# Exchanged attention products from the second batch on, with the exchange undone in the normalisation instead of in a second copy of the weights

## The chip, the cores and the metric

The kernel runs on one core of one Trainium2 chip. The metric is the time of one execution on the device, in microseconds. The engines are called as the profile calls them: PE (matrix products), PEld (its weight loads), ACT (activation functions), DVE (elementwise work and reductions), POOL (here mostly the issue of loads, and small elementwise work) and SP (a queue of DMA transfers). PSUM is the accumulator memory that PE writes and DVE and ACT read.

## The reference

Two layers, one behind the other. The first is an attention with a band of 32 positions to either side and 8 global positions, for 8 batches, 8 heads, 576 positions and a head dimension of 64. The second is a feed-forward layer over the 4608 tokens, with the width 512 and the inner width 2048.

```python
scores = scale * np.matmul(q, k.transpose(0, 1, 3, 2))
mask = np.abs(pos[:, None] - pos[None, :]) <= window
mask = mask | is_global[:, None] | is_global[None, :]
scores = np.where(mask, scores, -1000000000.0)
attn = softmax(scores)                      # along the keys
x = np.matmul(attn, v)                      # -> (4608, 512), heads side by side
h = x @ w_in                                # 512 x 2048
s = np.sin(alpha * h)
g = h + s * s / (alpha + 1e-09)
return (g @ w_out).astype(np.float32)       # 2048 x 512
```

## The kernel before, in words

Work goes batch by batch. For a batch `b` there is an attention stage (`attention(b)`), a first matrix stage (`gemm1(b)`, x times w_in with the sine part) and a second one (`gemm2(b)`, g times w_out). The order on every engine is the order in which the program is written out: `attention(b + 1)` follows `gemm1(b)`, and the matmuls of `gemm2` are handed out one by one by `fill(n)` between the pieces of both, to keep PE occupied. No scheduler moves anything.

In the attention two heads form a pair: one on partitions 0 to 63, one on 64 to 127. A batch has four pairs. The 576 queries are in two halves (positions 0 to 287 and 288 to 575, in each the even ones ahead of the odd ones); each half has its own PSUM bank, so that a product tile has two banks (half 0 and half 1) of 288 queries. For each pair `hp` the program writes, in this order:

- three groups of scores on PE (L740, into the two tiles of `ring`), the exponential on ACT (L748) and the mask on DVE (L751), with `fill` between the groups;
- between the second and the third group, the products of the pair before: `denominators` (L807, with a matrix of ones) into the tile `zd`, and the value products (L834) into the tile `zn`. Both are made of matmuls with 64 rows and 64 columns. For the last pair of a batch the values go into `zd` and the denominators into `zr`;
- after the third group, for the pair before: `inverse` on ACT (L860 the logarithm, L863 the exponential of its negative, into `R`), `sums` on DVE (L844, what the global rows need), and `normalise` on DVE (L866): values times `R`, from PSUM into `xT` in bfloat16.

The tiles `zn` and `zd` exist once each, so the next pair's products can be written only when the pair before has been read. `xT` has one chunk of 128 partitions for each pair, and `gemm1` takes the four chunks as its four contraction steps, the last pair's chunk last.

A *crossed* batch (`cross`) exchanges the heads of a pair in half 1: the product of the head on rows 0 to 63 goes to columns 64 to 127 and the other way round, while half 0 stays as it is:

```python
at = t ^ (half if cross else 0)
```

So the four quadrants of the PE array all have work, where a plain batch uses two. In the kernel before, batches 4 to 7 are crossed (`CROSS = 4`). For half 1 their `xT` holds the two heads in each other's places, and `gemm1` multiplies that half with `w_alt`, a copy of `w_in` whose two partition halves are exchanged. The copy is made by eight DMA transfers on SP's queue during the attention of batches 3 and 4.

The global rows of a batch are collected from `GS`, the output of `sums`, by `keep_globals` (L883, L885) and `finish_globals` (L893, L898) into extra columns of `xlast`. In a crossed batch other than the last the additions and the two last steps are on POOL and `finish_globals` is put off to the end of `gemm1`; otherwise all is on DVE. In a crossed batch the swap for half 1 is undone for these columns' sums and done again for the result.

Of the kernel before, what the change touches and what calls it, by code (L numbers as in the profile page):

```python
# [10 lines left out]
ALU = mybir.AluOpType  # L11
AF = mybir.ActivationFunctionType
DT = mybir.dt
# [3 lines left out]
P = 128  # L17
KW = 96
NG = 8
KT = 48  # L20
# [227 lines left out]
def kernel(  # L248
# [11 lines left out]
    nc = tc.nc  # L260
# [37 lines left out]
    HG = main.tile([P, NT, NG * B], DT.bfloat16, name="HG")  # L298
    identb = main.tile([P, P], DT.bfloat16, name="identb")
    ones = main.tile([P, P], DT.bfloat16, name="ones")  # L300
    w_alt = main.tile([P, CT, DFF], DT.bfloat16, name="w_alt")
    MASK = main.tile([P, NT12, WCOL], DT.bfloat16, name="MASK")
    kTg = main.tile([P, NHP, NG, B], DT.bfloat16, name="kTg")
    qTg = main.tile([P, NHP, NG, B], DT.bfloat16, name="qTg")
# [408 lines left out]
    def attention(b, beside):  # L713
# [139 lines left out]
        def body(hp, key):  # L853
            return nd(hp, key).rearrange("p k x c -> p (k x) c")[:, :, 0 : 3 * SEG].rearrange(
                "p k (m c) -> p k m c", c=SEG
            )[:, :, :, 4:]

        def inverse(hp):
# [3 lines left out]
            n = b * NHP + hp  # L862
            nc.scalar.activation(out=Rs[hp][:], in_=L[:], func=AF.Exp, scale=-1.0, accum_out=RA[:, n : n + 1])  # L863

        def normalise(hp):
            nc.vector.tensor_tensor(  # L866
                out=xT[:, hp, :, 0:HALF].rearrange("p e (k m c) -> p e k m c", k=2, c=KT) if odd
                else xT[:, hp].rearrange("p e (k m c) -> p (e k) m c", k=2, c=KT),
                in0=body(hp, 0).rearrange("p (e k) m c -> p e k m c", k=2) if odd else body(hp, 0),
                in1=Rs[hp][:].rearrange("p (e k) m c -> p e k m c", k=2) if odd else Rs[hp][:], op=ALU.mult,  # L870
            )
# [3 lines left out]
        SWAP = [(slice(0, D), slice(D, P)), (slice(D, P), slice(0, D))]  # L875

        def keep_globals(hps):

# [12 lines left out]
        def finish_globals(hps):  # L891

            nc.vector.reciprocal(out=RG[:, hps], in_=GT[:, 1, hps])  # L893
            to = xlast[:, hps, :, HALF:].rearrange("p h e (c x b) -> p h e x c b", x=2, b=B)
            for e in range(2):
                cs = slice(2 * e, 2 * e + 2)
                for mine, other in SWAP if e else [(slice(0, P), slice(0, P))]:
                    (nc.gpsimd if cross and not wide else nc.vector).tensor_tensor(  # L898
                        out=to[mine, :, e, :, :, b], in0=GT[other, 0, hps, :, cs], in1=RG[other, hps, :, cs],
                        op=ALU.mult,  # L900
                    )

        start, per_scores = (START, PER_SCORES) if b != 1 else (0, LATE)
        def idle(hp):
# [134 lines left out]
    def gemm1(b):  # L1039


        xT = xTs[b]
        r0 = (b % 2) * S
        more = b == B - 1
        W = HALF + (NE if more else 0)
        hr = tc.alloc_tile_pool(name="hr", bufs=1, space=PSUM)
        hs = {}

        order = "nrdonrdonrdnrdon" if b == 0 else "nrd" * 5 + "n"

        def chunks(nt, cs):
            if nt not in hs:
                if order[nt] == "o":
                    hs[nt] = [(slice(e, e + 1), zo[e][:, None, :]) for e in range(2)]
                else:
                    h = {"n": zn, "d": zd}.get(order[nt]) or hr.tile([P, 2, 512], DT.float32, name="zr")
                    hs[nt] = [(slice(0, 2), h[:])]
            h = [ap[:, i] for es, ap in hs[nt] for i in range(es.stop - es.start)]
            for c in cs:
                for e in range(2):  # L1060
                    lhsT = (w_alt if e and b >= CROSS else w_in)[:, c, nt * P : (nt + 1) * P]
                    nc.tensor.matmul(  # L1062
                        out=h[e][:, 0:W], lhsT=lhsT, rhs=xT[:, c, e, 0:W],
                        start=(c == 0), stop=(c == CT - 1), skip_group_check=True,
                    )

        on_act = (ON_ACT_FIRST, ON_ACT_SECOND, ON_ACT)[min(b, 2)]
        for nt in range(NT):
            if b < 2 and 10 <= nt < 14:
                for which, t, y in PLACES[2 * (nt - 10) : 2 * (nt - 9)]:  # L1070
                    place(b + 1, which, t, y, nc.vector.tensor_copy, slice(0, NHP if b else 2))
            if 1 < b < B - 1 and nt in ((3, 5, 7, 9) if b == 2 else (3, 5)):
                place(b + 1, *PLACES[(nt + 5 if b == 2 else nt + 9) // 2], nc.vector.tensor_copy)
            if b == 1 and nt == 14:
                turn_qk(3)
            if b == 1 and nt in (3, 4):
                square_x(0, nt - 3)
            if b == 0 and nt == 11:
                turn_kq()
            if b == 0 and nt == 11:  # L1080

                load_w_out()
                cast_globals_v()
                place_globals(1)
                load_v(1, (2, 3))
                load_vg(1)
            if nt == 0:

                for n in range(2):
                    chunks(n, range(CT - 1))  # L1090
            chunks(nt, range(CT - 1, CT) if nt < 2 else range(CT))
            fill((GROUP_LATE if b == 1 else PER_GROUP)[nt])
            sb = spool.tile([P, 2, HALF + NE], DT.bfloat16, name="sb")
            s2 = spool.tile([P, 2, HALF + NE], DT.bfloat16, name="s2")
            for es, h in hs[nt]:
                nc.scalar.activation(  # L1096
                    out=sb[:, es, 0:W], in_=h[:, :, 0:W], func=AF.Sin, scale=alphaT[:, nt : nt + 1]
                )
            if nt in on_act:
                nc.scalar.activation(out=s2[:, :, 0:W], in_=sb[:, :, 0:W], func=AF.Square)  # L1100
            else:
                nc.vector.tensor_tensor(out=s2[:, :, 0:W], in0=sb[:, :, 0:W], in1=sb[:, :, 0:W], op=ALU.mult)  # L1102
            for es, h in hs[nt]:
                nc.vector.scalar_tensor_tensor(  # L1104
                    out=H2[:, nt, r0 : r0 + S].rearrange("p (e c) -> p e c", e=2)[:, es],
                    in0=s2[:, es, 0:HALF], scalar=recipT[:, nt : nt + 1], in1=h[:, :, 0:HALF],
                    op0=ALU.mult, op1=ALU.add,
                )
            if more:
                nc.vector.scalar_tensor_tensor(  # L1110
                    out=HG[:, nt, :].rearrange("p (x n) -> p x n", x=2),
                    in0=s2[:, :, HALF:W], scalar=recipT[:, nt : nt + 1], in1=hs[nt][0][1][:, :, HALF:W],
                    op0=ALU.mult, op1=ALU.add,
                )
        if b and later:
            later.pop()()
        hr.release()
# [54 lines left out]
            else:  # L1172
                n -= 1

    CROSS = 4
    EXCHANGE = {(CROSS - 1, 0): 0, (CROSS - 1, 2): 1, (CROSS, -1): 2, (CROSS, 1): 3}
    START = 2
    PER_SCORES = ((1, 11, 3), (3, 2, 4), (3, 3, 3), (3, 4, 4))

# [12 lines left out]
    def phase_a(b_att, b_moe):  # L1192
        def beside(at):

            if b_moe is None:
                if at == -1:
                    nc.vector.tensor_scalar(out=recipT[:], in0=alphaT[:], scalar1=1e-9, scalar2=None, op0=ALU.add)
                    nc.vector.reciprocal(out=recipT[:], in_=recipT[:])
                if at == 0:
                    second_half()  # L1200
                    nc.gpsimd.memset(VX[1][:].bitcast(DT.int32), 0)
                    nc.gpsimd.memset(QX[1][:].bitcast(DT.int32), 0)
                    nc.gpsimd.memset(KX[1][:].bitcast(DT.int32), 0)
                    turn_qk(1)
                    nc.gpsimd.tensor_copy(out=seen[:], in_=turned[1][1][0:1, 0:1])
                    load_w_in((2, 3))
                    load_v(1, (0, 1))
                    gather(v, gv)
                return
            if 0 <= at < 2 and b_moe:  # L1210
                square_x(b_moe, at)
            if b_att == 1 and at == 0:
                place_rest(1)
                place_rest(0)
            for which, t, y in places_at(b_att, at):
# [12 lines left out]

        if b_moe is not None:
            waiting.append(gemm2(b_moe))  # L1230
        attention(b_att, beside)
# [83 lines left out]
```

## Time and profile before

| | |
|---|---|
| runs shown, median (lowest to highest) | 367.36 us (366.95 to 370.75) |
| the profiled execution's own time | 367.21 us |
| its span | 365.4 us |
| granted TensorE clock, mean | 0.995 |
| PE busy | 333.7 us, 91% of the span |
| ACT busy | 292.7 us, 80% |
| DVE busy | 286.0 us, 78% |
| POOL busy | 143.6 us, 39% |
| all normalisations (L866), 32 instructions | 24.2 us |

A row of a timeline gives the start in us, the duration in us, the engine, the line, the operation, the tile it writes and those it reads, the shape and how many instructions the row merges; in brackets stands how long the engine sat idle before it and which instruction ended that. A row of groups gives the total busy time in us and the mean in ns of one instruction. A row of windows gives the stretch, its length, and the busy time and the number of instructions of each engine in it. The busy time of PE contains modelled ends, so PE can look full while it waits.

### The profile page before, as it was taken

How to read it: one execution, taken by the hardware profiler on the slowest of the kernel's cores; microseconds unless marked ns; L12 is line 12 of the kernel's file. 1: busy time of each engine (PE TensorE's matmuls, PEld its weight loads, DVE VectorE, ACT ScalarE, POOL GpSimd, SP SyncE). 2: the span in 40 equal slices, each digit the busy share in tenths (PEclk: the TensorE clock that was granted, in tenths of full speed). 3: DMA queues.
4: the chain of work that ended last, by engine and by line, in shares of the span. 5: the costliest groups of instructions: out<-in, count | busy, mean ns of one | idle time of the engine just before them, and what ended most of it. 6: DMA issues, size and time to landing. Idle time of an engine off the chain costs nothing. (4 is left out here: it accounts for less than half of the span.)

```text
span 365.4 us, 9492 instructions
## 1 busy us (share of the span) xinstructions
PE 333.7 (91%) x3516; PEld 218.6 (60%) x3568; DVE 286.0 (78%) x630; ACT 292.7 (80%) x566; POOL 143.6 (39%) x264
## 2 busy tenths in 40 slices
PE   2579878999999999999999999999999999999993
PEld 2457655666666666676656765667566655565452
DVE  5775899698878888888886888698887878788751
ACT  5689898787879878887989788979888789778711
POOL 7992577479774700762004571294100010000001
PEclk9999999999999999999999999999999999999997
DMA  7999999999999885999244993198521001100321
GB/s 125 110 169 180 170 137 170 175 139 201 171 213 205 98 122 136 158 152 168 67 104 67 180 152 69 33 87 96 111 54 35 1 31 60 31 1 2 86 88 50
DMA packets 104222, 40.23 MB, mean 110 GB/s; under 512 B 94266, under 2 KB 98378, under 8 KB 103722
## 3 DMA queue, kind: packets, MB, share of 16 engines
q0 software_dynamic: 56640, 18.56, 44.5%
q1 hardware_dynamic: 47530, 20.99, 29.8%
q8 instruction: 30, 0.49, 0.6%
q14 instruction: 22, 0.18, 0.2%
HBM read 37.15 MB, written 17.83 MB: 150 GB/s over the span
## 5 line engine op out<-in xcount | busy, mean ns | idle before, releaser
L1125 PE MATMUL zo<-w_out,H 128*128 128x512 bf16 x524 | 141.4, 379 | 1.9 <-issue 0.2
L394 POOL DMA_DIRECT2D VX<-in_v_dram x128 | 83.5, 665 | 52.1 <-PE zn L834 19.5
L1062 PEld LDWEIGHTS <-w_in 128*128 128x128 bf16 x768 | 74.8, 98 | 36.2 <-issue 7.2
L1125 PEld LDWEIGHTS <-H 128*128 128x128 bf16 x576 | 52.3, 97 | 37.4
L748 ACT ACTIVATE E<-ring 128x480 bf16<-128x480 f32 x96 | 54.4, 569 | 19.5 <-PE ring L740 19.3
L751 DVE TENSOR_TENSOR E<-E,MASK 128x480 bf16<-128x480 bf16 x96 | 36.1, 406 | 13.0 <-ACT E L748 11.1
L1104 DVE SCALAR_TENSOR_TENSOR H<-s,recipT,zn 128x576 bf16<-128x576 bf16 x47 | 38.2, 814 | 8.8 <-ACT s L1100 4.8
L1100 ACT ACTIVATE s<-sb 128x576 bf16<-128x576 bf16 (+1 forms) x62 | 42.8, 691 | 2.0
L740 PE MATMUL ring<-QX,KX 128*128 128x120 bf16 x384 | 37.4, 222 | 6.9 <-ACT E L748 2.6
L1096 ACT ACTIVATE sb<-zn,alphaT 128x576 bf16<-128x576 f32 (+1 forms) x47 | 34.9, 742 | 10.8 <-PE zn L1062 9.6
L740 PEld LDWEIGHTS <-KX 128*128 128x128 bf16 x384 | 27.4, 100 | 23.5 <-issue 6.8
L1102 DVE TENSOR_TENSOR s<-sb 128x576 bf16<-128x576 bf16 (+1 forms) x66 | 30.6, 464 | 10.4 <-ACT sb L1096 10.3
L1104 DVE SCALAR_TENSOR_TENSOR H<-s,recipT,zr 128x576 bf16<-128x576 bf16 x39 | 31.7, 814 | 4.9 <-ACT s L1100 2.6
L1104 DVE SCALAR_TENSOR_TENSOR H<-s,recipT,zd 128x576 bf16<-128x576 bf16 x39 | 31.7, 813 | 4.5 <-ACT s L1100 2.4
L1096 ACT ACTIVATE sb<-zd,alphaT 128x576 bf16<-128x576 f32 (+1 forms) x39 | 28.9, 742 | 7.8 <-PE zd L1062 7.6
L1096 ACT ACTIVATE sb<-zr,alphaT 128x576 bf16<-128x576 f32 (+1 forms) x39 | 28.9, 742 | 6.5 <-PE zr L1062 6.4
L1062 PEld LDWEIGHTS <-w_alt 128*128 128x128 bf16 x256 | 25.0, 98 | 13.2 <-issue 4.0
L1131 ACT COPY osb<-zo 128x512 f32<-128x512 f32 x36 | 20.8, 579 | 12.6 <-PE zo L1125 11.5
L1062 PE MATMUL zn<-xlast,w_in 128*128 128x288 bf16 (+1 forms) x144 | 27.0, 288 | 0.6 <-DVE xlast L898 0.3
L1062 PE MATMUL zn<-xT,w_in 128*128 128x288 bf16 x136 | 25.2, 286 | 2.2 <-DMA w_in<-in_moe_w_in_dram 1.6
L807 PEld LDWEIGHTS <-ones 64*64 64x64 bf16 x512 | 17.5, 107 | 15.9 <-issue 12.0
L1159 POOL DMA_INDIRECT out_dram<-osb,ghalf x1 | 1.1, 1106 | 63.7 <-POOLq L1283 63.7
(170 smaller groups left out, 556.5 us busy)
## 6 DMA issues: line engine op xcount, KB each, us to landing
VX<-in_v_dram POOLq DMA_DIRECT2D x128, 36.0 KB, 5.8
kd<-in_k_dram POOLq DMA_DIRECT2D x7, 576.0 KB, 6.8
qd<-in_q_dram POOLq DMA_DIRECT2D x7, 576.0 KB, 10.0
w_in<-in_moe_w_in_dram POOLq DMA_DIRECT2D x4, 512.0 KB, 6.9
w_out<-in_moe_w_out_dram POOLq DMA_DIRECT2D x4, 512.0 KB, 7.9
out_dram<-osb SPq DMA_DIRECT2D x8, 256.0 KB
w_alt<-w_in SPq DMA_DIRECT2D x8, 256.0 KB
out_dram<-osb SPq DMA_DIRECT2D x8, 224.0 KB
```

Of the source, the lines that this page charges most:

```text
L394: nc.gpsimd.dma_start(out=VX[b % 2][r : r + 24, hp], in_=v[b, 2 * hp + t].rearrange("(i a y) d -> y a i d", a=24, y=2)[y],)
L740: nc.tensor.matmul(out=ps[:, e * WCOL : (e + 1) * WCOL], lhsT=kx[:, hp, i, :], rhs=qx[:, hp, :, s0 : s0 + 60], start=True, stop=True, skip ...
L748: nc.scalar.activation(out=Eg, in_=ps[:, 0 : 4 * WCOL], func=AF.Exp, scale=scale, accum_out=EA[:, n : n + 1])
L751: nc.vector.tensor_tensor(out=Eg, in0=Eg, in1=MASK[:, 4 * g : 4 * g + 4, :].rearrange("p i c -> p (i c)"), op=ALU.mult,)
L807: nc.tensor.matmul(out=bass.AP(tensor=to.tensor, offset=to.offset, ap=[list(to.ap[0]), [SEG, len(ms)], list(to.ap[1]), [1, hi - lo]],), lh ...
L1062: nc.tensor.matmul(out=h[e][:, 0:W], lhsT=lhsT, rhs=xT[:, c, e, 0:W], start=(c == 0), stop=(c == CT - 1), skip_group_check=True,)
L1096: nc.scalar.activation(out=sb[:, es, 0:W], in_=h[:, :, 0:W], func=AF.Sin, scale=alphaT[:, nt : nt + 1])
L1100: nc.scalar.activation(out=s2[:, :, 0:W], in_=sb[:, :, 0:W], func=AF.Square)
L1102: nc.vector.tensor_tensor(out=s2[:, :, 0:W], in0=sb[:, :, 0:W], in1=sb[:, :, 0:W], op=ALU.mult)
L1104: nc.vector.scalar_tensor_tensor(out=H2[:, nt, r0 : r0 + S].rearrange("p (e c) -> p e c", e=2)[:, es], in0=s2[:, es, 0:HALF], scalar=recip ...
L1125: nc.tensor.matmul(out=ops[:], lhsT=H2[:, nt, blk * P : (blk + 1) * P], rhs=w_out[:, nt, :], start=(nt == 0), stop=(nt == NT - 1),)
L1131: nc.scalar.copy(out=osb[:], in_=ops[:])
```

## The change

`w_alt` and its eight transfers are gone, and `gemm1` uses `w_in` for both halves. `CROSS` is 1, so the batches 1 to 7 are crossed. `normalise` in a crossed batch is written as three instructions in place of one: one over all partitions for half 0, and two over 64 partitions each for half 1, which read one partition half and write the other, so that `xT` has both heads where they belong. `finish_globals` has two instructions in place of three in the crossed batches, since nothing needs to be exchanged there any more. With `CROSS`, `keep_globals` and the last steps of `finish_globals` of the batches 1 to 3 move from DVE to POOL, and the last steps to the end of `gemm1`.

```diff
-    w_alt = main.tile([P, CT, DFF], DT.bfloat16, name="w_alt")
...
+        SAME = [(slice(0, P), slice(0, P))]
+        SWAP = [(slice(0, D), slice(D, P)), (slice(D, P), slice(0, D))]
+
         def normalise(hp):
-            nc.vector.tensor_tensor(
-                out=xT[:, hp, :, 0:HALF]...,
-                in0=body(hp, 0)..., in1=Rs[hp][:]..., op=ALU.mult,
-            )
+            if not cross:
+                nc.vector.tensor_tensor(
+                    out=xT[:, hp, :, 0:HALF]...,
+                    in0=body(hp, 0)..., in1=Rs[hp][:]..., op=ALU.mult,
+                )
+                return
+            for e in range(2):
+                ks = slice(2 * e, 2 * e + 2)
+                for mine, other in SWAP if e else SAME:
+                    nc.vector.tensor_tensor(
+                        out=xT[mine, hp, e, 0:HALF].rearrange("p (k m c) -> p k m c", k=2, c=KT),
+                        in0=body(hp, 0)[other, ks], in1=Rs[hp][other, ks], op=ALU.mult,
+                    )
...
             for e in range(2):
                 cs = slice(2 * e, 2 * e + 2)
-                for mine, other in SWAP if e else [(slice(0, P), slice(0, P))]:
-                    (nc.gpsimd if cross and not wide else nc.vector).tensor_tensor(
-                        out=to[mine, :, e, :, :, b], in0=GT[other, 0, hps, :, cs], in1=RG[other, hps, :, cs],
-                        op=ALU.mult,
-                    )
+                (nc.gpsimd if cross and not wide else nc.vector).tensor_tensor(
+                    out=to[:, :, e, :, :, b], in0=GT[:, 0, hps, :, cs], in1=RG[:, hps, :, cs], op=ALU.mult
+                )
...
-                    lhsT = (w_alt if e and b >= CROSS else w_in)[:, c, nt * P : (nt + 1) * P]
+                    lhsT = w_in[:, c, nt * P : (nt + 1) * P]
...
-    CROSS = 4
-    EXCHANGE = {(CROSS - 1, 0): 0, (CROSS - 1, 2): 1, (CROSS, -1): 2, (CROSS, 1): 3}
+    CROSS = 1
...
-            if (b_att, at) in EXCHANGE:
-                c = EXCHANGE[b_att, at]
-                for t in range(2):
-                    nc.sync.dma_start(
-                        out=w_alt[t * D : (t + 1) * D, c], in_=w_in[(1 - t) * D : (2 - t) * D, c]
-                    )
```

More of the change, by code (lines that the diff above doesn't have):

```diff
@@ L863, in inverse @@
             nc.scalar.activation(out=Rs[hp][:], in_=L[:], func=AF.Exp, scale=-1.0, accum_out=RA[:, n : n + 1])
+        SAME = [(slice(0, P), slice(0, P))]
+        SWAP = [(slice(0, D), slice(D, P)), (slice(D, P), slice(0, D))]
         def normalise(hp):
[L866 to L870, printed above, removed]
-            )
+            if not cross:
+                nc.vector.tensor_tensor(
+                    out=xT[:, hp, :, 0:HALF].rearrange("p e (k m c) -> p e k m c", k=2, c=KT) if odd
+                    else xT[:, hp].rearrange("p e (k m c) -> p (e k) m c", k=2, c=KT),
+                    in0=body(hp, 0).rearrange("p (e k) m c -> p e k m c", k=2) if odd else body(hp, 0),
+                    in1=Rs[hp][:].rearrange("p (e k) m c -> p e k m c", k=2) if odd else Rs[hp][:], op=ALU.mult,
+                )
[7 more added lines that the diff above has]
+                    )
         GT, GM = [normp.tile([P, 2, NHP, 2, 4], DT.float32, name=name) for name in ("GT", "GM")]
         RG = normp.tile([P, NHP, 2, 4], DT.float32, name="RG")
-        SWAP = [(slice(0, D), slice(D, P)), (slice(D, P), slice(0, D))]
         def keep_globals(hps):
```

## The prediction

> **What bounds the kernel now.** I read the page first, for the span, then the busy time of each engine over the attention stages, then the timeline of two of those stages side by side: batch 3, the last one whose products are not exchanged, and batch 6, one of those whose products are.
>
> ```profile
> span 365.4 us, 9492 instructions
> ...
> core 0: us, PE busy (x) PEld busy (x) DVE busy (x) ACT busy (x) POOL busy (x), PEclk, DMA share, GB/s
> 137.84:157.49 19.65, 19.28 (x272) 12.37 (x275) 15.46 (x37) 16.30 (x41) 8.35 (x13) 1.00 0.78 141
> 178.04:196.18 18.14, 17.70 (x272) 10.35 (x275) 15.37 (x37) 16.48 (x41) 0.00 (x0) 1.00 0.29 76
> 254.88:273.04 18.16, 17.73 (x273) 10.35 (x276) 15.39 (x36) 16.05 (x40) 1.17 (x3) 1.00 0.42 82
> 96.79:116.92 20.13, 19.76 (x274) 12.63 (x277) 14.90 (x35) 16.31 (x42) 13.59 (x26) 1.00 1.25 201
> ```
>
> The stretches are the attention of batches 3, 4, 6 and 2. PE looks full in all, yet its busy time holds modelled ends, so the timeline decides. Batches 4 and 6 take the same time within 0.02 us; I let batch 6 stand for 4 and 5. Exchanged attention is 1.49 us shorter than plain attention (19.65 against 18.16).
>
> ```profile
> 143.73 0.79 PE L807 MATMUL zd<-E,ones 64*64 64x264 bf16 x16
> 144.35 0.79 PE L834 MATMUL zn<-E,VX 64*64 64x88 bf16 x28
> 147.64 0.76 DVE L866 TENSOR_TENSOR xlast<-zn,R 128x576 bf16<-128x576 f32 x1 [0.45 <-ACT R L863]
> 148.60 0.79 PE L834 MATMUL zn<-E,VX 64*64 64x88 bf16 x28
> 152.84 0.79 PE L834 MATMUL zn<-E,VX 64*64 64x88 bf16 x28
> 157.49 0.90 PE L1062 MATMUL zn<-xlast,w_in 128*128 128x288 bf16 x6
> ...
> 260.78 0.49 PE L807 MATMUL zd<-E,ones 64*64 64x264 bf16 x16
> 261.10 0.48 PE L834 MATMUL zn<-E,VX 64*64 64x88 bf16 x28
> 261.51 0.38 PE L740 MATMUL ring<-QX,KX 128*128 128x120 bf16 x4
> 261.93 0.57 ACT L748 ACTIVATE E<-ring 128x480 bf16<-128x480 f32 x1 [0.81 <-PE ring L740]
> 262.49 0.74 ACT L860 ACTIVATE L<-zd,tiny 128x576 f32<-128x576 f32 x1
> 263.26 0.68 ACT L863 ACTIVATE R<-L 128x576 f32<-128x576 f32 x1
> 263.26 0.23 DVE L844 TENSOR_REDUCE GS<-zd 128x16 f32<-128x64 f32 x1 [0.22 <-ACT L L860]
> 263.40 0.21 DVE L844 TENSOR_REDUCE GS<-zn 128x16 f32<-128x64 f32 x1
> 264.07 0.76 DVE L866 TENSOR_TENSOR xT<-zn,R 128x576 bf16<-128x576 f32 x1 [0.45 <-ACT R L863]
> 264.74 1.24 DVE L992 TENSOR_TENSOR SQ<-SQ 128x1152 bf16<-128x1152 bf16 x2
> 264.88 0.60 PE L834 MATMUL zn<-E,VX 64*64 64x88 bf16 x28
> 267.93 0.21 DVE L844 TENSOR_REDUCE GS<-zn 128x16 f32<-128x64 f32 x1
> 268.06 0.75 DVE L866 TENSOR_TENSOR xT<-zn,R 128x576 bf16<-128x576 f32 x1
> 268.86 0.60 PE L834 MATMUL zn<-E,VX 64*64 64x88 bf16 x28
> 273.04 0.29 PE L1062 MATMUL zn<-xT,w_in 128*128 128x288 bf16 x1
> ```
>
> The reader is to see a closed loop in batch 6. The value products (L834) write the one tile zn; the third group of scores (L740) follows on PE; ACT takes its exponential (L748), then the logarithm and the reciprocal of the denominators (L860, L863); DVE normalises out of zn (L866); only then may the next value products overwrite zn. From 261.10 on each begins within some 0.1 us of the end of the one before, and 264.07 + 0.76 = 264.83 is followed by value products at 264.88; again 268.06 + 0.75 = 268.81 and 268.86. The loop takes 3.78 us, then 3.98 us. In batch 3 the normalisation ends at 148.40 and the products begin at 148.60, when PE comes to them by itself: there PE is the bound, with 4.25 and 4.24 us from products to products. So **in the exchanged batches the normalisation is on the path that sets the end, in the plain ones it has 0.2 us to spare.** The change makes all batches from 1 on exchanged ones, and makes just this instruction longer.
>
> **The change, part by part.** *The normalisation.* One instruction over 576 elements becomes three over 288: all partitions for the first half, and two of 64 partitions for the second. No 288-wide form of it is in this trace. Its price comes from another PSUM operation that occurs in both widths:
>
> ```profile
> L866 DVE TENSOR_TENSOR xT<-zn,R 128x576 bf16<-128x576 f32 x12 | 9.1, 755 | 4.1 <-ACT R L863 4.1
> ...
> L1104 DVE SCALAR_TENSOR_TENSOR H<-s,recipT,zn 128x576 bf16<-128x576 bf16 x47 | 38.2, 814 | 8.8 <-ACT s L1100 4.8 <-PE zd L1062 0.5 <-issue 0.2
> ...
> L1104 DVE SCALAR_TENSOR_TENSOR H<-s,recipT,zo 128x288 bf16<-128x288 bf16 x6 | 2.8, 508 | 0.1
> ...
> L898 DVE TENSOR_TENSOR xlast<-GT,RG 64x8 bf16<-64x8 f32 x4 | 0.8, 190 | 0.1
> ...
> 308.08 0.60 DVE L898 TENSOR_TENSOR xlast<-GT,RG 128x8 bf16<-128x8 f32 x3
> ```
>
> Half the width saves 814 - 508 = 306 ns, so one piece takes about 755 - 306 = 449 ns; that only half of the partitions take part saves nothing, I assume. Do the pieces overlap? The two sums at 263.26 and 263.40 do: each lasts over 0.2 us and they start 0.14 us apart, 0.09 us of overlap. The L898 triple at 308.08 is one full-width piece and two that swap the partition halves: 0.60 us against 3 x 0.19, so 0.015 us of gap each and no overlap. The new triple has that shape, so I take no overlap: 3 x 0.45 + 2 x 0.015 = 1.38 us against 0.755, **0.63 us later at its end**. The instruction behind it also loses its overlap (SQ started at 264.74, before 264.83): 0.10 us of DVE more. Lower bound, with overlap: 3 x 0.45 - 2 x 0.09 = 1.17, +0.42 us. Upper bound, pieces as dear as the 508 ns row: 1.55, +0.80 us.
>
> The Trainium skill (VectorE: DVE Perf Modes, section on two Vector instructions with no wait between them) says that an instruction is held until all earlier Vector instructions have finished if its inputs or its output start in another 32-partition quadrant than the last ones did. By that rule both swapped pieces and the instruction after them are held, and the triple at 308.08 agrees with it, at no overlap. The section on the errata of that page gives 120 cycles plus one per element at 0.96 GHz for a PSUM source: by that estimate 425 ns a piece, 725 ns for the whole (the trace has 755), and a total near 374 us.
>
> *Batches 4 to 6.* The first loop grows by 0.63. In the second DVE has no spare time between the two normalisations (the last sum ends at 268.14, behind the start at 268.06), so the lost overlap counts too: 0.73. Then the first matrix product needs the last normalisation:
>
> ```profile
> 273.88 0.76 DVE L866 TENSOR_TENSOR xT<-zd,R 128x576 bf16<-128x576 f32 x1 [0.46 <-ACT R L863]
> ...
> 274.81 0.28 PE L1062 MATMUL zn<-xT,w_alt 128*128 128x288 bf16 x1
> ```
>
> The second half of the last chunk began at 274.81; it now waits until 273.88 + 1.38 + 0.05 = 275.31: 0.50. PE takes its work in a fixed order, so fill-in matmuls queued behind the waiting one can't cover it. Sum 1.86 a batch, **5.6 us**.
>
> *Batch 7.* Two loops at 0.63 (DVE has no SQ work there). Its gathering of the global rows stands on DVE ahead of the last normalisation:
>
> ```profile
> 312.43 0.62 DVE L898 TENSOR_TENSOR xlast<-GT,RG 128x8 bf16<-128x8 f32 x3
> 313.07 0.76 DVE L866 TENSOR_TENSOR xlast<-zd,R 128x576 bf16<-128x576 f32 x1
> 314.18 0.30 PE L1062 MATMUL zn<-xlast,w_alt 128*128 128x320 bf16 x1
> ```
>
> The triple at 312.43 loses one piece (0.2 us) and the one at 308.08 as well; the normalisation of the third pair ahead of it is longer by 0.63 and 0.10. So 313.07 moves by 0.53, its end comes at 314.98, and the product of 314.18 begins at 315.03, 0.85 late; less the 0.2 of the earlier triple, 0.65. **1.9 us.**
>
> *Batches 1 to 3* become exchanged. The denominators shrink from 0.62 (143.73 to 144.35) to 0.32 (260.78 to 261.10): -0.30. The loops become 3.78 + 0.63 = 4.41 against 4.25 and 3.98 + 0.73 = 4.71 against 4.24: +0.16 and +0.47. From the last value products into zn to the matrix product it is 4.18 (268.86 to 273.04) against 4.65 (152.84 to 157.49): -0.47. The wait for the last normalisation adds about 0.45. Together +0.31 a batch, taken three times: **0.9 us**. Half of PE's gain is given back in each loop.
>
> *What costs nothing.* Eight copies of w_in go from SP's queue; nobody waits for them until batch 4. The global rows of batches 1 to 3 move from DVE to POOL, where the copy GM waits for the sums at the end of the attention, with the casts and V loads of later batches queued behind it:
>
> ```profile
> 102.99 0.53 POOL L331 DMA_DIRECT2D kd<-in_k_dram  x1
> ...
> 126.14 2.63 POOL L394 DMA_DIRECT2D VX<-in_v_dram  x4
> 145.44 2.55 POOL L394 DMA_DIRECT2D VX<-in_v_dram  x4 [16.67 <-PE zn L834]
> ```
>
> At worst, in batch 2, the cast of 102.99 (for batch 4) waits for the end of that attention at 116.92, some 14 us, and with it the loads that ended at 128.77. But POOL then stood idle for 16.67 us, and the transpose that needs the cast is issued when the next matrix stage ends, at 137.84, some 20 us after the late cast. If that cover were short, batch 4's keys would be late by the difference. I take 0.
>
> **Sum.** 5.6 + 1.9 + 0.9 = 8.4 us on the profiled execution's own 367.2 us (its span of 365.4 and 1.8 around it; the median of the runs is 367.36, which is the same): **375.6 us**, 2.2% slower.
>
> **Rivals.** *The pieces overlap.* With 0.42 in place of 0.63 and nothing lost behind it: batches 4 to 6 3.4 (0.42 + 0.42 + 0.29 each), batch 7 1.0, batches 1 to 3 -1.3 (-0.30 - 0.05 + 0.16 - 0.47 + 0.24 each): 3.1 us, 370.3 us. For it speaks the overlap at 263.40; against it the triple at 308.08.
>
> *The exchange pays and the pieces are hidden.* If the value products started when the old normalisation would have ended (because the pieces run shorter, or only the first gates them), batches 1 to 3 would each gain the 1.49 us between the windows: 367.2 - 4.5 = 362.7 us. It decides from the point where the triple takes no longer than 0.76 + 0.2 us. Against it: the same products of batch 6 start 0.05 us after the whole normalisation. The Trainium skill (TensorEngine Tiling, on the PSUM bottleneck) has the rule behind this: packing the array speeds up TensorE but not the emptying of PSUM. The 0.05 us agree with it.
>
> *DVE becomes the bound.* It is busy 15.4 of 18.2 us in such a stage and gets 4 x 0.73 = 2.9 more: 18.3. If its order then delays the masks that all products need, all 2.9 us land on the path in seven batches, less the 4.5: 367.2 + 20.4 - 4.5 = 383.1 us. Against it: while PE waits, DVE's later work moves along with PE's.
>
> **How the numbers follow.** Forecast 0.70, overlap 0.15, hidden pieces 0.05, DVE bound 0.10. The upper bound of 0.80 us gives batches 4 to 6 7.1, batch 7 2.6, batches 1 to 3 2.5: 379.4 us. The range is 370.3 to 379.5. About 1% is what the measurement can tell from no change (363.7 to 371.0): the forecast and the DVE case lie above, half of the overlap case within. Faster 0.04, same 0.09, slower 0.87.
>
> **What would show it.** Right: triples of about 0.45 us each and 1.38 together; value products 0.05 us behind the third piece in every batch from 1 on, 4.4 and 4.7 us apart; exchanged denominators of 0.32 us from batch 1; attention stages of about 19.5 us; the second half of the first matrix product behind the last piece. Wrong: value products that start ahead of the third piece, pieces that overlap, or gaps on PE that the profile puts to POOL's loads.

## The result, and the profile after

The changed kernel takes 379.25 us (median of 6 runs, 377.54 to 380.94) where the kernel before, run beside it, takes 369.65 (366.95 to 373.83): the ratio is 1.028 with a 95% interval of 1.021 to 1.034. It is taken from the means without one run of the kernel before (373.83 us), which fell in a slower state. The forecast was 375.6 us, or +8.4; measured is +9.6 between the medians and +10.3 between the means behind the ratio. The profiled execution took 379.52 us.

The page of the changed kernel:

```profile
span 377.8 us, 9530 instructions
...
PE 332.9 (88%) x3516; PEld 213.6 (57%) x3568; DVE 299.2 (79%) x671; ACT 291.9 (77%) x566; POOL 148.6 (39%) x276
```

PE's work is as it was; the span is 12.4 us longer and DVE is busy for 13 us more. The windows of the changed kernel, with the columns of the ones shown before, over the attention of batches 3, 4, 6 and 2:

```profile
140.89:162.36 21.47, 18.41 (x272) 10.52 (x275) 17.42 (x43) 16.35 (x41) 6.19 (x14) 1.00 0.65 88
183.17:203.07 19.90, 17.91 (x273) 10.36 (x275) 17.34 (x43) 16.81 (x43) 1.99 (x4) 1.00 0.37 66
263.72:283.71 19.99, 18.00 (x273) 10.45 (x275) 17.33 (x43) 16.35 (x41) 0.81 (x2) 1.00 0.39 72
99.14:119.87 20.73, 18.44 (x275) 10.60 (x277) 16.98 (x41) 16.38 (x43) 5.91 (x11) 1.00 0.54 89
```

Batches 4 and 6 grow from 18.14 and 18.16 us to 19.90 and 19.99. Batch 2, which gained the cheaper products, still goes from 20.13 to 20.73, and batch 3 from 19.65 to 21.47. The timeline of batch 6 in the changed kernel:

```profile
273.00 1.39 DVE L879 TENSOR_TENSOR xT<-zn,R 128x288 bf16<-128x288 f32 x3 [0.45 <-ACT R L862]
...
274.42 1.25 DVE L1000 TENSOR_TENSOR SQ<-SQ 128x1152 bf16<-128x1152 bf16 x2
274.44 0.60 PE L833 MATMUL zn<-E,VX 64*64 64x88 bf16 x28 [0.61 <-DVE xT L879]
...
277.74 1.38 DVE L879 TENSOR_TENSOR xT<-zn,R 128x288 bf16<-128x288 f32 x3
279.18 0.60 PE L833 MATMUL zn<-E,VX 64*64 64x88 bf16 x28 [0.82 <-DVE xT L879]
...
282.26 1.39 DVE L879 TENSOR_TENSOR xT<-zn,R 128x288 bf16<-128x288 f32 x3 [0.45 <-ACT R L862]
...
283.71 0.90 PE L1070 MATMUL zn<-xT,w_in 128*128 128x288 bf16 x6 [0.20 <-DVE xT L879]
...
284.18 1.41 DVE L879 TENSOR_TENSOR xT<-zd,R 128x288 bf16<-128x288 f32 x3
...
285.65 0.28 PE L1070 MATMUL zn<-xT,w_in 128*128 128x288 bf16 x1 [0.18 <-DVE xT L879]
```

Each row of L879 is the three pieces together. The value products follow 0.05 and 0.06 us behind the last piece, and PE is now idle in front of them with DVE's normalisation as releaser, which before it was not. The last but one PE row is a wait that the prediction didn't name: the first matmul of the matrix product writes `zn` too, and waits for the third pair's normalisation (282.26 + 1.39 = 283.65).

To place the loss, I take in each batch the start of the second half of the last chunk in the first matrix product (285.65 above, 274.81 before), and the steps from batch to batch:

| batch | before, us | after, us | step longer by |
|---|---|---|---|
| 0 | 35.36 | 35.09 | |
| 1 | 74.44 | 76.81 | 2.64 |
| 2 | 118.52 | 121.57 | 0.68 |
| 3 | 159.08 | 164.30 | 2.17 |
| 4 | 197.78 | 204.77 | 1.77 |
| 5 | 236.28 | 245.12 | 1.85 |
| 6 | 274.81 | 285.65 | 2.00 |
| 7 | 314.18 | 326.72 | 1.70 |

Batches 4 to 7 sum to 7.3 us against 7.5 forecast; batches 1 to 3 to 5.5 against 0.9. Three parts make up most of the surplus. In batch 1 most is a wait in the matrix stage before it, for the load of `w_in`. The changed kernel's timeline:

```profile
44.14 2.10 PE L1070 MATMUL zn<-xT,w_in 128*128 128x288 bf16 x8 [2.35 <-DMA w_in<-in_moe_w_in_dram]
```

That stage (the first matrix product of batch 0) lasted 21.82 us, and 19.77 before. In the twelve experiments below it took 17.8 to 22.3 us, from 17.8 to 22.1 among the variants of the kernel before alone: the scatter of one load, not the change. It accounts for 2.05 of the 2.64 us.

In batch 2 it is a second loop of 5.10 us. The changed kernel's DVE in it:

```profile
110.22 1.25 DVE L1000 TENSOR_TENSOR SQ<-SQ 128x1152 bf16<-128x1152 bf16 x2
...
111.73 0.91 DVE L356 COPY KX<-kt 64x1152 bf16<-64x1152 bf16 x2
112.67 1.05 DVE L750 TENSOR_TENSOR E<-E,MASK 128x480 bf16<-128x480 bf16 x3
...
113.91 1.38 DVE L879 TENSOR_TENSOR xT<-zn,R 128x288 bf16<-128x288 f32 x3
```

DVE has no gap worth the name there and two key copies (L356) where the same loop of batch 6 has one. The loop is 0.36 us longer than the 4.74 us (274.44 to 279.18) of batch 6, which the prediction let stand for it; that the second copy makes the difference is read from these rows.

Batch 3 is the part that the prediction had set to zero. POOL, SP, DVE and PE in the changed kernel's timeline, in order of time:

```profile
120.33 0.51 POOL L893 COPY GM<-GS 64x64 f32<-64x64 f32 x2 [14.34 <-DVE GS L843]
...
121.18 0.59 POOL L330 DMA_DIRECT2D kd<-in_k_dram  x1
...
143.93 2.56 POOL L393 DMA_DIRECT2D VX<-in_v_dram  x4
```

```profile
122.63 9.74 SPq L402 DMA_DIRECT2D VX<-VGb  x8
...
134.65 6.27 SPq L339 DMA_TRANSPOSE kt<-kd  x1
141.02 4.77 SPq L339 DMA_TRANSPOSE qt<-qd  x1
```

```profile
146.28 0.96 DVE L356 COPY KX<-kt 64x1152 bf16<-64x1152 bf16 x2 [2.47 <-DMA kt<-kd]
147.27 1.05 DVE L750 TENSOR_TENSOR E<-E,MASK 128x480 bf16<-128x480 bf16 x3
148.05 0.73 PE L806 MATMUL zd<-E,ones 64*64 64x264 bf16 x12 [1.05 <-DVE E L750]
```

And SP in the kernel before:

```profile
119.76 6.14 SPq L403 DMA_DIRECT2D VX<-VGb  x8
...
131.56 3.20 SPq L340 DMA_TRANSPOSE kt<-kd  x1
134.88 2.55 SPq L340 DMA_TRANSPOSE qt<-qd  x1
```

`GM` waits for the end of batch 2's attention, and with it the cast at 121.18, which before was issued at 102.99. The V loads whose issue used to end at 128.77 are now issued until 146.49, so SP's two transposes run beside loads from POOL's queue, and their rows last 6.27 and 4.77 us instead of 3.20 and 2.55. DVE comes to its key copy 2.47 us before the keys have landed; masks and denominators stand behind it, and PE has 1.05 us of idle time in front of the denominators. From the last matmul of the matrix stage to the first value products (the head of a batch, below) it is 7.81 us, 6.64 before, and 6.34 in the exchanged batches 4 and 6.

### The profile page after: what moved, and what is told of

Read it like the earlier page. It is cut to its first block, busy times and chain, and to the rows that moved or that the text cites. A ratio compares the mean times of both kernels' runs of the same rounds, so it can differ in the third digit from the quotient of the medians.

```text
span 377.8 us, 9530 instructions
## 1 busy us (share of the span) xinstructions
PE 332.9 (88%) x3516; PEld 213.6 (57%) x3568; DVE 299.2 (79%) x671; ACT 291.9 (77%) x566; POOL 148.6 (39%) x276
## 5 line engine op out<-in xcount | busy, mean ns | idle before, releaser
L1070 PEld LDWEIGHTS <-w_in 128*128 128x128 bf16 x1024 | 99.7, 98 | 54.6 <-issue 15.0
L393 POOL DMA_DIRECT2D VX<-in_v_dram x128 | 83.5, 664 | 32.8 <-DMA qd<-in_q_dram 10.3
L1104 ACT ACTIVATE sb<-zn,alphaT 128x576 bf16<-128x576 f32 (+1 forms) x47 | 34.8, 740 | 15.3 <-PE zn L1070 15.3
L1104 ACT ACTIVATE sb<-zd,alphaT 128x576 bf16<-128x576 f32 (+1 forms) x39 | 28.9, 740 | 7.9 <-PE zd L1070 7.9
L893 POOL COPY GM<-GS 64x64 f32<-64x64 f32 x12 | 3.3, 274 | 79.9 <-DVE GS L843 79.7
L1104 ACT ACTIVATE sb<-zr,alphaT 128x576 bf16<-128x576 f32 (+1 forms) x39 | 28.9, 740 | 7.2 <-PE zr L1070 7.0
L1070 PE MATMUL zn<-xT,w_in 128*128 128x288 bf16 x184 | 28.3, 293 | 3.7 <-DMA w_in<-in_moe_w_in_dram 2.3
L1070 PE MATMUL zn<-xlast,w_in 128*128 128x288 bf16 (+1 forms) x192 | 29.5, 289 | 2.2 <-DVE xlast L879 1.2
L833 PEld LDWEIGHTS <-VX 64*64 64x64 bf16 x896 | 17.5, 109 | 13.4 <-issue 13.3
```

Source lines behind the costliest of these rows:

```text
L393: nc.gpsimd.dma_start(out=VX[b % 2][r : r + 24, hp], in_=v[b, 2 * hp + t].rearrange("(i a y) d -> y a i d", a=24, y=2)[y],)
L833: nc.tensor.matmul(out=out_t[at * D : (at + 1) * D, half, :, a - half * CUT : z - half * CUT], lhsT=VXb[rows, hp, i, :], rhs=E[rows, i, :, ...
L1070: nc.tensor.matmul(out=h[e][:, 0:W], lhsT=lhsT, rhs=xT[:, c, e, 0:W], start=(c == 0), stop=(c == CT - 1), skip_group_check=True,)
L1104: nc.scalar.activation(out=sb[:, es, 0:W], in_=h[:, :, 0:W], func=AF.Sin, scale=alphaT[:, nt : nt + 1])
```

## The experiments

"Before" below is the kernel before run on the same chip beside each experiment (medians 368.71, 368.75 and 368.02 us in the three groups of four). Loops are counted from the start of one pair's value products to the next's.

### The changed kernel, exchanging from batch 4

```diff
-    CROSS = 1
+    CROSS = 4
```

> The changed kernel with the exchange from batch 4 on again (batches 1 to 3 plain, with one normalisation instruction and their global rows on DVE); w_alt stays out and batches 4 to 7 keep the three-piece normalisation. My theory (the longer normalisation lies in the loop of products and normalisation): batches 4 to 7 cost 7.3 us as in the profile after (1.8, 1.9, 2.0, 1.7 from the second half of one first matrix product to the next), batches 1 to 3 nothing: about +7.5 us on the kernel before, and no DVE wait for the key transposes in batch 3. Rival (the exchange in the early batches is what costs, through DVE's total load or the tiles' new addresses): about +3 us or less. Rival (new addresses alone): as slow as the changed kernel, +10.

Measured: 374.88 us, ratio 1.017 (1.013 to 1.021). In the profile the steps of batches 4 to 7 are 40.47, 40.32, 40.66 and 41.07 us, together 7.4 longer than before, and those of batches 1 to 3 are as before within 0.3 us (39.09, 44.06, 40.89). So in the profile the pieces cost what was forecast for them, and the rest is in batches 1 to 3. Between the medians it is 6.2 us (4.9 to 7.6 by the interval).

### The changed kernel with the old layout of memory

```diff
+    w_alt = main.tile([P, CT, DFF], DT.bfloat16, name="w_alt")
```

> The changed kernel with the tile w_alt still allocated and not used, so that all tiles lie where they lay in the kernel before. My theory (addresses play no part; the 2 us that the first matrix stage of batch 0 took longer in the profile after, waiting for w_in, are chance): as slow as the changed kernel within 1 us, about 2.7% slower than the kernel before. Rival (the shift of the tiles by 16 KB slows the transposes and the loads of batch 0): 2 us faster than the changed kernel, and the first matrix stage of batch 0 takes 19.8 us again instead of 21.8.

Measured: 378.6 us, ratio 1.027 (1.023 to 1.031), and the stages are those of the changed kernel, 7.82 us at the head of batch 3 included. No effect of the addresses is seen. Beside the run above on the same chip, it puts a number on batches 1 to 3 that doesn't hang on one profile: 378.6 - 374.88 = 3.7 us.

### The changed kernel with the global rows of batches 1 to 3 on DVE

```diff
-            eng = nc.gpsimd if cross and not wide else nc.vector
+            eng = nc.gpsimd if cross and not wide and b >= 4 else nc.vector
```

(and the same condition at the two other places, L896 and L907)

> The changed kernel, but the global rows of batches 1 to 3 are collected and finished on DVE at once, as in the kernel before; POOL has only its loads there. My theory of the part that I missed (POOL holds the casts and loads of batches 4 and 5 until the sums of batch 2 are there, so the key transposes of batch 4 come late and DVE waits 2.5 us for them in batch 3, with the masks queued behind): this wait goes, batch 3 gets about 1.2 us faster than in the changed kernel, the whole 0.5 to 1.5 us, since DVE has some 1.4 us more at the end of three batches. Rival (the transposes are slow because of the traffic or the addresses, not because of POOL's order): the wait stays and the time is the same or slower.

Measured: 377.29 us, ratio 1.024 (1.020 to 1.028). Its profile, SP in batch 3:

```profile
124.25 6.15 SPq L402 DMA_DIRECT2D VX<-VGb  x8
...
136.42 2.93 SPq L339 DMA_TRANSPOSE kt<-kd  x1
```

The transposes are short again (that of the queries takes 2.01 us), DVE has no wait for the keys in the view of waits, and the head of batch 3 takes 6.34 us instead of 7.81. So the move to POOL is what made batch 3 late: 1.47 us there. In the runs only 1.3 of 3.7 us come back (378.6 to 377.29; the intervals overlap), since the rows on DVE delay the sine part: the matrix stage of batch 2 takes 21.44 us instead of 20.91.

### Three pieces for the first pair alone, and for the third alone

The kernel before, where one chunk of `xT` is written unexchanged in three pieces and multiplied with `w_in`:

```diff
+    THREE = (0,)        # (2,) in the second kernel
...
+            if cross and hp in THREE:
+                ... three pieces as in the change
...
-                    lhsT = (w_alt if e and b >= CROSS else w_in)[:, c, nt * P : (nt + 1) * P]
+                    lhsT = (w_alt if e and b >= CROSS and c not in THREE else w_in)[:, c, nt * P : (nt + 1) * P]
```

> The kernel before (exchange from batch 4 on, w_alt kept), with the three-piece normalisation for the first pair only of batches 4 to 7; the first chunk of the product then takes w_in for both halves, and the global rows have one more small instruction. My theory (place decides: the next value products wait for this normalisation): first to second value products 4.4 us instead of 3.8, the others as before, +0.65 to +0.75 us a batch, +2.8 us in all. Rival (DVE's load decides): the same cost for the first and the third pair.

> As the run before it, with the three pieces for the third pair only. No value products wait for this pair's normalisation; only the first matmul of the matrix stage does, which uses the same PSUM tile and had 0.3 us to spare. My theory: third value products to matrix stage 4.5 us instead of 4.2, all else as before, +0.35 us a batch and some 0.5 in batch 7 (global rows), +1.5 us in all, half of the first pair's cost. Rival (DVE's load decides): the same as for the first pair, +2.8 us.

Measured: 371.72 us, ratio 1.008 (1.005 to 1.012), and 371.3 us, 1.006 (1.003 to 1.010). The times alone can't tell the two apart; the profiles can. The first pair alone, batch 6:

```profile
266.85 1.39 DVE L873 TENSOR_TENSOR xT<-zn,R 128x288 bf16<-128x288 f32 x3 [0.26 <-ACT R L863]
...
268.29 0.60 PE L834 MATMUL zn<-E,VX 64*64 64x88 bf16 x28 [0.62 <-DVE xT L873]
...
272.40 0.60 PE L834 MATMUL zn<-E,VX 64*64 64x88 bf16 x28 [0.19 <-DVE xT L878]
```

The loop with the three pieces takes 4.41 us, the one behind it 4.11 (268.29 to 272.40) instead of 3.98: 0.63 and 0.13, as the prediction had it with 0.63 and 0.10. The steps of batches 4 to 7 grow by 0.69, 0.73, 0.74 and 0.64, 2.8 us in all. The third pair alone, batch 6:

```profile
271.90 0.60 PE L834 MATMUL zn<-E,VX 64*64 64x88 bf16 x28
...
274.99 1.40 DVE L873 TENSOR_TENSOR xT<-zn,R 128x288 bf16<-128x288 f32 x3 [0.45 <-ACT R L863]
...
276.43 0.28 PE L1081 MATMUL zn<-xT,w_in 128*128 128x288 bf16 x1 [0.20 <-DVE xT L873]
```

Both loops stay at 3.77 and 3.98, and the matrix product starts 4.53 us behind the value products (271.90 to 276.43) instead of 4.18. The steps grow by 0.53, 0.41, 0.15 and 0.43, 1.5 us in all. So the wait of the matrix product for `zn` is real, and the third pair pays for its pieces there.

### Three pieces that exchange nothing

The kernel before, with each exchanged batch's normalisation in three pieces whose output is on the partitions of the input:

```diff
+            if cross:
+                for e, rows in ((0, slice(0, P)), (1, slice(0, D)), (1, slice(D, P))):
+                    ks = slice(2 * e, 2 * e + 2)
+                    nc.vector.tensor_tensor(
+                        out=xT[rows, hp, e, 0:HALF]...,
+                        in0=body(hp, 0)[rows, ks], in1=Rs[hp][rows, ks], op=ALU.mult,
+                    )
+                return
```

> The kernel before, with every normalisation of batches 4 to 7 in three pieces of the same sizes that don't change partitions: all partitions, 0 to 63, 64 to 127; w_alt kept. By the Trainium skill's rule on held Vector instructions (VectorE: DVE Perf Modes) the second piece is not held and the third one is: 0.45 + 0.45 + 0.45 - 0.09 + 0.015, 1.28 us, against 1.39 us for the exchanging pieces. If the exchange itself cost something, the pieces would be shorter than 0.45 us. If pieces never overlap whatever their partitions, 1.39 us. Loops 0.5 us longer than in the kernel before, +6 us in all.

Measured: 373.96 us, ratio 1.014 (1.008 to 1.020). Three views of one triple in its timeline (the first window ends behind the first piece, the second begins ahead of the second piece, the third holds all three), and the group's rows (64 and 128 partitions):

```profile
269.44 0.46 DVE L869 TENSOR_TENSOR xT<-zn,R 128x288 bf16<-128x288 f32 x1 [0.45 <-ACT R L863]
```

```profile
269.82 0.91 DVE L869 TENSOR_TENSOR xT<-zn,R 64x288 bf16<-64x288 f32 x2
```

```profile
269.44 1.29 DVE L869 TENSOR_TENSOR xT<-zn,R 128x288 bf16<-128x288 f32 x3 [0.45 <-ACT R L863]
```

```profile
L869 DVE TENSOR_TENSOR xlast<-zn,R 64x288 bf16<-64x288 f32 x12 | 5.4, 450 | 0.1
...
L869 DVE TENSOR_TENSOR xlast<-zn,R 128x288 bf16<-128x288 f32 x6 | 2.7, 456 | 1.6 <-ACT R L863 1.5
```

The second piece starts at 269.82, 0.08 us before the first has ended (269.90). The two 64-partition pieces take 0.91 us, twice the group's mean of 450 ns and a gap. The whole is 1.29 us where the exchanging triple takes 1.38 to 1.41. The Trainium skill (VectorE: DVE Perf Modes, section on two Vector instructions with no wait between them) holds an instruction back whose inputs or output start in another 32-partition quadrant than the last ones. By that rule the second piece here isn't held and the third is, and this trace agrees: one overlap of 0.08, then none. The missing overlap is worth about 0.1 us. The other 0.53 of the 0.63 us (1.29 against 0.76) is the splitting itself. The loops are 4.30 and 4.75: the first is 0.11 us shorter than with the exchanging pieces, the second (4.74 there) is not, and why isn't settled.

### The inverse ahead of the third scores, in the changed kernel and in the kernel before

```diff
             elif hp:
                 products(hp - 1)
+                inverse(hp - 1)
             scores(hp, 2)
...
             if hp:
-                inverse(hp - 1)
+                if b == 0:
+                    inverse(hp - 1)
```

> The changed kernel, with logarithm and reciprocal of a pair issued ahead of the third group of scores' exponential on ACT (batches 1 to 7), so that the loop from value products over scores, exponential, logarithm, reciprocal and normalisation to the next value products is cut: logarithm and reciprocal need the denominators only. My theory (the normalisation costs what it costs only because it ends this loop): it starts about 1 us earlier after the value products, the loops of 4.4 and 4.7 us shrink to 3.7 to 4.1, and the changed kernel gains 4 to 8 us; the third exponential comes 1.4 us later, which may make the scores wait for their PSUM tile and take back a part. Rival (DVE's load or PE's waits for masks decide): gain below 1 us.

> The kernel before with logarithm and reciprocal issued ahead of the third exponential, as in the last run. In the changed kernel that move left the two loops at 4.38 and 4.74 us (DVE now has the mask and the sums ahead of the normalisation) and shortened the end of the attention by 0.6 us. My theory: here the loops of batches 4 to 7 fall to 4.38 - 0.63 = 3.75 and about 4.0, no gain, and the end of the attention gains 0.2 to 0.5 us a batch: 1 to 3 us faster than the kernel before, ratio 0.992 to 0.998. Rival (the later exponential delays scores and masks by more): 1 to 3 us slower.

Measured: the changed kernel takes 374.16 us, ratio 1.016 (1.011 to 1.021), some 4 us less than without this. The kernel before takes 369.3 us with it, 1.005 (1.001 to 1.008). The changed kernel with the edit, batch 6:

```profile
266.57 0.68 ACT L862 ACTIVATE R<-L 128x576 f32<-128x576 f32 x1
...
267.25 0.55 ACT L747 ACTIVATE E<-ring 128x480 bf16<-128x480 f32 x1
...
267.92 0.41 DVE L750 TENSOR_TENSOR E<-E,MASK 128x480 bf16<-128x480 bf16 x1 [0.49 <-ACT E L747]
...
268.51 1.38 DVE L879 TENSOR_TENSOR xT<-zn,R 128x288 bf16<-128x288 f32 x3
...
269.95 0.60 PE L833 MATMUL zn<-E,VX 64*64 64x88 bf16 x28 [0.57 <-DVE xT L879]
...
273.25 1.39 DVE L879 TENSOR_TENSOR xT<-zn,R 128x288 bf16<-128x288 f32 x3
```

The reciprocal is ready at 267.25 (266.57 + 0.68), but the normalisation starts at 268.51, behind the mask and the sums in DVE's order. The loops stay at 4.38 and 4.74 us, against what was expected. The exponential isn't out of the first loop: it now comes behind the reciprocal on ACT (267.25), the mask waits for it (DVE idle for 0.49 us), and the normalisation stands behind the mask on DVE. So the same three steps on ACT are still ahead of the normalisation, in another order. In the second loop DVE works without a pause, as in the changed kernel. The gain is at the end of the attention, where the matrix product comes 3.94 us behind the value products instead of 4.53. In the kernel before the same edit makes that stretch longer, 4.41 us for 4.18: ACT takes logarithm and reciprocal first, so the exponential, and with it the last pair's products, come later.

### Both repairs in the changed kernel

The edit above, and the global rows of batches 1 to 3 on DVE.

> The changed kernel with both mends: logarithm and reciprocal first, and the global rows of batches 1 to 3 on DVE. The two are in different places, so their gains should add: 4 us of the one and 1 to 1.5 us of the other, 373 us against 379, ratio to the kernel before 1.012; the wait for key transposes in batch 3 is gone (last matmul of the matrix stage to first value products 6.3 us, not 7.8). Rival (both take the same slack): no faster than the first mend alone, 1.016.

Measured: 372.02 us, ratio 1.011 (1.006 to 1.017). The head of batch 3 is 6.34 us, the loops stay at 4.38 and 4.74. In the profile both gains are there, as expected: the one at the head, the other at the end of the attention (3.92 us instead of 4.53). The times alone don't decide it: 1.016, the first repair alone, still lies inside the interval. The two loops are as long as they were.

### The kernel before, exchanging earlier with its copy of the weights

If the exchanged products are worth 1.5 us a batch without the pieces, the old method may gain from starting earlier. The first of three tries is one number:

```diff
-    CROSS = 4
+    CROSS = 2
```

> The kernel before with CROSS = 2: the exchanged copy w_alt stays and is made two batches earlier, batches 2 to 7 are exchanged, the normalisation is one instruction everywhere. My theory (the exchange shortens an attention stage by 1.5 us as long as the normalisation is one instruction): batches 2 and 3 gain 1.5 us each, so -3 us, less up to 1 us if the global rows on POOL delay the transposes of batch 4: 364 to 366 us where the kernel before has 367. Rival (the early batches are held by DVE or by transfers, so the exchange can't pay there): no change within 1 us.

Measured: 369.14 us, ratio 1.000 (0.997 to 1.004). Its waits, and SP at the time:

```profile
DVE KX L357 <- DMA kt<-kd: 5.3, 3, 2.8
```

```profile
83.11 1.23 SPq L1225 DMA_DIRECT2D w_alt<-w_in  x2
...
85.33 12.67 SPq L403 DMA_DIRECT2D VX<-VGb  x8
...
100.07 4.73 SPq L340 DMA_TRANSPOSE kt<-kd  x1
```

The transpose of the keys that DVE copies during batch 2's attention starts at 100.07, where it started at 93.47. On SP's queue it stands behind two copies into `w_alt` and behind the eight transfers of `VX<-VGb`, which take 12.67 us here and 6.99 before. That the copies slow these transfers is read from the order of the queue and was not tried by itself. The second loop of batch 2 grows to 6.25 us, from 4.24. In batch 3, whose forerunner's global rows are now on POOL as in the change, the head takes 8.07 us.

The next two start at batch 3 and keep the global rows of that batch on DVE; the second of them leaves the inverse in its place.

> The best version that the runs point to: w_alt and the single normalisation kept, exchange from batch 3 on, its global rows in batch 3 on DVE, logarithm and reciprocal first. My theory: 1.5 us from batch 3's exchange and 1 to 3 us from the order on ACT: 363 to 366 us, ratio 0.987 to 0.995. Rival (the eight copies, now in batches 2 and 3, again run into the key transposes, as they did one batch earlier): no gain from the exchange, ratio 0.995 to 1.0.

> The same without the new order on ACT: exchange from batch 3 on with w_alt, global rows of batch 3 on DVE. My theory: batch 3's attention takes 18.2 us as in batches 4 to 6 instead of 19.8, ratio 0.996, no wait for key transposes. Rival (copies collide with the transposes): a wait of 1 to 3 us in batch 2 or 3 and a ratio of 1.0 or above, as with the exchange from batch 2 on.

Measured: 368.31 us, ratio 0.999 (0.996 to 1.002), and 368.4 us, 1.000 (0.997 to 1.003). Neither gains. Waits for the keys don't explain it: in the view of waits DVE waits for them once in the first (0.9 us) and never in the second. With the inverse first, the step of batch 3 is 1.1 us shorter (39.43 for 40.57), and the plain batches, whose attention ends 0.4 us later, and batches 4 and 5 (0.20 and 0.55 us) give it back. Without it, that step is 1.15 us shorter, and the next is 1.16 longer. There the profile of this kernel shows:

```profile
158.75 0.76 DVE L866 TENSOR_TENSOR xlast<-zd,R 128x576 bf16<-128x576 f32 x1 [0.45 <-ACT R L863]
...
159.54 0.62 DVE L883 COPY GM<-GS 64x64 f32<-64x64 f32 x2
...
161.04 1.15 DVE L898 TENSOR_TENSOR xlast<-GT,RG 128x16 bf16<-128x16 f32 x3
...
162.91 0.81 DVE L1104 SCALAR_TENSOR_TENSOR H<-s,recipT,zn 128x576 bf16<-128x576 bf16 x1
...
163.78 0.28 PE L1062 MATMUL zn<-xlast,w_in 128*128 128x288 bf16 x1 [1.08 <-DVE H L1104]
```

An exchanged batch has two copies into `GM` and a longer last step for its global rows. On DVE they stand ahead of the sine part: from the last normalisation to the first L1104 it takes 4.16 us (158.75 to 162.91), 3.10 in the kernel before (158.04 to 161.14), and PE waits 1.08 us. On POOL the rows hold up the casts, on DVE the sine part. Of the versions tried, none beats the kernel before.

## Why the prediction was right or wrong

*The three pieces: right.* A piece takes 0.45 us, the three 1.38 to 1.41, without overlap. The rival with overlapping pieces fell, and so did the one in which the pieces are hidden: PE waits for DVE in front of each of the value products shown.

*Batches 4 to 7: the sum right, one step in the wrong place.* In the profile 5.6 us were forecast and 5.6 found for batches 4 to 6, 1.9 and 1.7 for batch 7. The prediction took the 4.18 us from the value products to the matrix product as unmoved and charged 0.50 to the last normalisation. In fact the first matmul already waits, for `zn`: 0.35 there (4.53 us), and 0.10 to 0.17 at the last chunk. The third pair's pieces alone showed it. That the two make up the 0.50 that was charged is luck.

*DVE as the bound: half true.* In the second loop DVE does work without a pause, and where 0.73 us were priced in for it, 0.76 came. The 2.9 us a batch of that rival did not.

*What costs nothing: wrong.* The step that failed is "I take 0" for the global rows on POOL. The prediction named the right wait, in the right batch, and the point from which it decides. It weighed only the lateness of the cast against the start of the transpose, and it put that start at 137.84, the end of the matrix stage; the trace of the kernel before has it at 131.56. The shorter cover still held: the transpose is issued 3.1 us later than before (134.65 and 131.56), which is how late the whole batch was (121.57 and 118.52). The prediction left out that the loads behind the cast on POOL would then run in the time of the transposes. That the rows on POOL are the cause is shown by taking them back: the head of batch 3 (the last matmul of the matrix stage to the first value products) goes from 7.81 to 6.34 us, 1.47 where the prediction has 0. That the loads lengthen the transposes is read from the traces: in the four profiles with batch 2's global rows on POOL this transpose of keys lasts 5.50 to 6.27 us, in the ten others 2.75 to 3.51. Which of the loads does it, V or the casts for batch 5, was not tried.

*Batches 1 to 3: the size was wrong.* 0.9 us was the term; 3.7 us is the difference of the runs with and without them. Of the 2.8 us between them, batch 3 has the 1.5 us just told, and batch 2 the 0.36 us for the second key copy that batch 6, its model, doesn't have. The wait for `zn` at the first matmul counts here too. The prediction credited 0.47 us a batch for a shorter way from the value products to the matrix product; the way went from 4.77, 4.70 and 4.65 us to 4.53, which is 0.24, 0.17 and 0.12. The last chunk cost 0.34, 0.10 and 0.35 where 0.45 was charged, so some 0.3 us of the surplus remain from this step. In batch 1 0.6 us are left in the profile shown once the wait for `w_in` is taken out. Of these 0.4 lie in its head and first loop, 10.50 us together for 10.09; but in the variants of the kernel before that exchange from batch 3 or 4 on, the same stretch takes 10.07 to 10.95, so the change isn't told from scatter there.

*The total.* Of the 3.65 us between 375.6 and 379.25, some 2 us are the kernel before: beside the changed kernel it took 369.1 us (the mean behind the ratio; the median of all six is 369.65), and 367.36 is the median of the three runs shown. The rest is the term of batches 1 to 3, 2.8 us more than forecast, less what batches 4 to 7 cost in the runs (6.2 us with an interval of 4.9 to 7.6, where 7.5 were forecast). So the forecast of +8.4 stands as near to the measured +9.6 as it does partly by luck: a term that was missed and one that came out smaller offset each other.

## What to carry to other kernels

Where one tile is written, read and written again, the reader's length can be on the path whatever its share of busy time; see which wait ends last there, and split the reader only if something is gained that stands in the same loop. When work moves to a queue that also issues loads, follow not only the first late load but all that it pushes into the time of other transfers. Price a batch by its own rows; a batch that stands for another must have the same number of each instruction in the loop.

## What had not been expected of the hardware

A VectorE instruction on 64 partitions took as long as one on 128: 450 against 456 ns for the same 288 elements, and 755 ns for 576 in one. Three small instructions in place of one thus cost 0.5 us even where nothing is exchanged. And a DMA transpose of the keys took 3.20 us in the kernel before and 6.27 in the changed one, where loads from POOL's queue ran beside it, with the same shape and place in SP's queue.
